# A gated-shift MLP block on one core: tiles 10 and 11 transposed by DMA, and the order around the second and third pair of tiles rewritten

## The chip, the cores and the metric

The kernel runs on one core of one Trainium2 chip. The metric is the time of one execution on the device in microseconds (us); lower is better. The core has five instruction streams that run side by side and wait for each other by semaphores: TensorE (PE in the profile, its weight loads PEld), VectorE (DVE), ScalarE (ACT), GpSimd (POOL) and SyncE (SP). SP issues nearly all DMAs here, ScalarE the first three.

## The reference

The input x has 2048 rows of 512; all data is bfloat16. Cut to what matters:

```python
h  = gelu(layernorm(x) @ w1)                 # w1: 512 x 512
hs = concat(h[:, 0:128]   shifted down 1 row,
            h[:, 128:256] shifted up 1 row,
            h[:, 256:384] shifted down 2 rows,
            h[:, 384:512] shifted up 2 rows) @ w2   # zeros come in at the ends
x1 = x + hs
out = x1 + gelu(layernorm(x1) @ w3) @ w4     # w3: 512 x 1792, w4: 1792 x 512
```

## The kernel before, in words

The rows are dealt to 16 tiles of 128 rows so that row r is row r // 16 of tile r % 16 (line 183). A shift by one or two rows is then a step to a neighbouring tile: for tile t the second product reads quarter j=0 of h from tile t-1, j=1 from t+1, j=2 from t-2 and j=3 from t+2 (`window`, lines 229 to 242). The layer norm is split in steps on three engines: `st` (statistics, VectorE, line 291), `ag` (mean and variance, VectorE, 296), `rs` (reciprocal roots, GpSimd, 302) and `nm` (the normalised tile, VectorE, 311). Every product needs its input transposed.

Every operation is recorded with a name, an engine, and what it reads and writes. `arrange` (lines 38 to 82) then puts the operations of each engine into the order of a list of names written by hand (`firsts`, lines 662 to 676), and `emit` (84 to 169) derives the semaphore waits. Each engine executes its list in order, so an operation that waits holds back all that stand behind it on its engine. That is true of SP too: a DMA whose source isn't ready holds back the later DMAs of the list.

The names, with the tile's number t (of a pair, the first tile):

- `ldx`, `ldw1`, `ldw2`, `ldw3a`, `ldw3b`, `ldw4`: loads of tiles of x (128 KB each) and of parts of the weights. `ldw20` to `ldw23` are the four 128-row parts of w2, one for each j; `ldw3a0` to `ldw3a3` are 256 KB each.
- Tiles 0 to 5 take a way of their own: `tp` and `ev` transpose the raw x on TensorE (line 357) and copy it out of the matmul accumulator banks, PSUM, on ScalarE (366), `m1r` is the first product (405), `rc` copies it out (415), `cs` and `cse` make the column sums of w1 (393, 397), and `zr` (420) and `g1r` (426) apply the norm afterwards. `th` transposes their h by DMA (384).
- Tiles 6 to 15, in pairs: the normalised tiles are transposed. Pairs 6, 12 and 14 do this with one DMA each (`td0_6`, `td0_12`, `td0_14`, line 377, issued on SP), pairs 8 and 10 with eight TensorE transposes (`tp8`, `tp10`, line 357) and a copy on ScalarE (`ev8`, `ev10`, line 366). Then `m1p` is the first product of a pair (16 matmuls of 256 columns, line 437, into two PSUM banks), and `g1p` or, for each tile of pair 10 alone, `g1s` is its GELU on ScalarE (447, 452).
- `m2` is the second product of a tile, four matmuls of 512 columns, one for each j (463). For tiles 8 to 13 it is cut in parts (`m2s`, line 478): parts ending in a letter come first, the part without a letter last. `x1` adds x on VectorE (488).
- The second layer: `st1`, `ag1`, `rs1`, `nm1` as above, `td1` transposes by DMA (377), `m3` and `m3h` are the third product (496, 520), `g2` and `g2h` its GELU (507, 531), `m4` the fourth (539), `fin` the last sum (551). It starts with tiles 8 to 11, the first call being `m3h_0_0_0` in banks 4 and 5.

The eight PSUM banks are given out by hand. Before the change m1p of the pairs 6, 8, 10, 12 and 14 uses the banks 2-3, 4-5, 0-1, 2-3 and 4-5, and the second products of the tiles 8 to 15 use 6, 7, 0, 1, 6, 7, 2, 3. `cs` is in bank 4, the `m1r` of tiles 4 and 5 in banks 0 and 1.

Of the kernel before, what the change touches and what calls it, by code (L numbers as in the profile page):

```python
# [5 lines left out]
P = 128  # L6
ACT_F = mybir.ActivationFunctionType
ALU = mybir.AluOpType
BF16 = mybir.dt.bfloat16
F32 = mybir.dt.float32  # L10
# [16 lines left out]
class Program:  # L27
# [7 lines left out]
    def add(self, eng, name, fn, reads=(), writes=(), dma=False):  # L35
        self.ops.append(Op(name, eng, fn, reads, writes, dma))
# [135 lines left out]
def bass_standalone__mixer_s_mlp__prompt_kernel(nc: bass.Bass, x, w1, w2, w3, w4, out):  # L172
# [3 lines left out]
    NT = S // P  # L176
# [9 lines left out]
    POS = {t: k for k, t in enumerate(ORDER)}  # L186

    with ExitStack() as es:
# [18 lines left out]
        st9 = sb("st9", [P, 2 * NT, 9], F32)  # L207
        mv = sb("mv", [P, 2 * NT, 2], F32)
        rstd = sb("rstd", [P, 2 * NT], F32)
        nmean = sb("nmean", [P, 2 * NT], F32)  # L210
        nbias = sb("nbias", [P, 2 * NT], F32)
        neghalf = sb("neghalf", [P, 4], F32)
        warm = sb("warm", [P, 1], F32)
        o_sb = sb("o_sb", [P, 4, D], BF16)
# [32 lines left out]
        add = pr.add  # L247
# [34 lines left out]
        def src_of(layer, t):  # L282
            return (x_sb, ("x", t)) if layer == 0 else (x1_sb, ("x1", t))

        def dst_of(layer, t):
            return (xn, t, ("xn", t), 0) if layer == 0 else (x1n, POS[t] % 8, ("x1n", POS[t] % 8), t)
# [19 lines left out]
        def norm(layer, t):  # L306
            src, r = src_of(layer, t)
            dst, k, dr, tag = dst_of(layer, t)
            i = layer * NT + (t if layer == 0 else POS[t])
            add("dve", f"nm{layer}_{t}",  # L310
                lambda e: e.tensor_scalar(dst[:, k, :], src[:, t, :], mv[:, i, 0:1], rstd[:, i : i + 1],  # L311
                                          ALU.subtract, ALU.mult),
                reads=[(r, 0), (("mv", i), 0), (("rstd", i), 0)], writes=[(dr, tag)])

        def nbias_op(layer, t, n):
            i = layer * NT + (t if layer == 0 else POS[t])
            add("dve", f"nb{layer}_{t}",
                lambda e: e.scalar_tensor_tensor(nbias[:, i : i + n], mv[:, i : i + n, 0], -1.0,
                                                 rstd[:, i : i + n], ALU.mult, ALU.mult),
                reads=[(("mv", i + k), 0) for k in range(n)] + [(("rstd", i + k), 0) for k in range(n)],  # L320
                writes=[(("nb", i + k), 0) for k in range(n)])

        def norm_act(layer, t):
            src, r = src_of(layer, t)
            dst, k, dr, tag = dst_of(layer, t)
            i = layer * NT + (t if layer == 0 else POS[t])
            add("act", f"na{layer}_{t}",
                lambda e: e.activation(dst[:, k, :], src[:, t, :], ACT_F.Identity,
                                       bias=nbias[:, i : i + 1], scale=rstd[:, i : i + 1]),
                reads=[(r, 0), (("nb", i), 0), (("rstd", i), 0)], writes=[(dr, tag)])  # L330

        def negmean(layer, t, n):
            i = layer * NT + (t if layer == 0 else POS[t])
            add("dve", f"ng{layer}_{t}",
                lambda e: e.tensor_scalar(nmean[:, i : i + n], mv[:, i : i + n, 0], -1.0, None, ALU.mult),
                reads=[(("mv", i + k), 0) for k in range(n)], writes=[(("nmean", i + k), 0) for k in range(n)])

        def norm_pool(layer, t):
            src, r = src_of(layer, t)
            dst, k, dr, tag = dst_of(layer, t)  # L340
            i = layer * NT + (t if layer == 0 else POS[t])
            add("pool", f"np{layer}_{t}",
                lambda e: e.tensor_scalar(dst[:, k, :], src[:, t, :], nmean[:, i : i + 1], rstd[:, i : i + 1],
                                          ALU.add, ALU.mult),
                reads=[(r, 0), (("nmean", i), 0), (("rstd", i), 0)], writes=[(dr, tag)])


        def tp(t, n, b, raw):
            src = x_sb if raw else xn
            rd = [(("x", i), 0) if raw else (("xn", i), 0) for i in range(t, t + n)]  # L350

            def f(e):
                ins = None
                for i in range(n):
                    for c in range(DC):
                        o = 1024 * b + (i * DC + c) * P
                        ins = e.transpose(psb[:, o : o + P], src[:, t + i, P * c : P * (c + 1)], ident[:])  # L357
                return ins

            add("pe", f"tp{t}", f, reads=rd + [("ident", 1)], writes=bres(b, 1, f"tp{t}"))  # L360
# [107 lines left out]
            add("pe", f"m2_{t}", f, reads=rd, writes=bres(b, 1, f"m2_{t}"))  # L468


        def m2s(t, b, js, first, last):
            wins = [(j, window(j, t)) for j in js]
            assert all(w[2] is None for _, w in wins)

            def f(e):
                ins = None
                for n, (j, w) in enumerate(wins):
                    ins = e.matmul(bank(b), hTf[:, w[0] : w[0] + P], w2_sb[:, j, :],  # L478
                                   start=first and n == 0, stop=last and n == len(js) - 1)
                return ins  # L480

            name = f"m2_{t}" if last else f"m2_{t}a" if first else f"m2_{t}b"
            add("pe", name, f, reads=[W2[j] for j in js] + [(("hT", w[1]), 0) for _, w in wins],
                writes=bres(b, 1, name))

# [100 lines left out]
        load_w1(2, "act")  # L586
        load_w1(3, "sp")
        load_x(1, 1, "act")
        for t, n in ((6, 1), (7, 1), (2, 1), (8, 1), (3, 1), (9, 1), (10, 1), (4, 1), (11, 1), (5, 1), (12, 2), (14, 1), (15, 1)):
            load_x(t, n)  # L590
        for c in range(DC):
            load_w2(c)
# [19 lines left out]
        for t in range(R, NT, 2):  # L612
            roots(0, t, 2)
        for t in range(R, NT):
            if t in ():
                nbias_op(0, t, 1)
                norm_act(0, t)
            else:
                norm(0, t)
        for t in range(R, NT, 2):  # L620
            if t in (8, 10):
                tp(t, 2, 6 + t // 2 % 2, False)
                ev(t, 2, 6 + t // 2 % 2)
            else:
                tdma(0, t, 2)
        for t, b in ((6, 2), (8, 4), (10, 0), (12, 2), (14, 4)):
            m1p(t, b)
            if t == 10:
                g1s(t, b, 0)
                g1s(t, b, 1)  # L630
            else:
                g1p(t, b)
        load_w("w4", w4_sb, w4, after=[(("x1T", 12), 0)])
        even = [((0, 1, 2), True, False), ((3,), False, True)]
        odd = [((0, 2), True, False), ((1, 3), False, True)]
        M2PARTS = {8: even, 9: [odd[0], ((1,), False, False), ((3,), False, True)], 10: even, 11: odd, 12: even, 13: odd}
        for t, b in ((8, 6), (9, 7), (10, 0), (11, 1), (12, 6), (13, 7), (14, 2), (15, 3)):
            for js, first, last in M2PARTS.get(t, ()):
                m2s(t, b, js, first, last)
            if t not in M2PARTS:  # L640
                m2(t, b)
            x1(t, b)
# [9 lines left out]
        for t in (8, 10):  # L652
# [8 lines left out]

        firsts = {}
        firsts["pe"] = """wu tp0 cs0 cs1 m1r01 m1r02 tp1 m1r03 m1r0 cs2 tp2 m1r12 m1r1 cs tp3 m1r2 tp4 m1r3 tp5 m1r4 m1r5 tp8 m1p6
            tp10 m1p8 m1p10 m2_8a m2_9a m2_8 m2_9b m2_9 m2_10a m2_11a m1p12 m1p14 m2_10 m2_11 m2_12a m2_13a m2_12 m2_13 m2_14 m2_15""".split()
        firsts["act"] = """ldw10 ldw12 ldx1 table ev0 ev1 ev2 rc0 ev3 rc1 ev4 rc2 ev5 rc3 rc4 rc5 ev8 cse g1p6 ev10 g1p8 g1s10 g1s11
            g1r0 g1r1 g1p12 g1p14 g2h_0_0_0 g2h_0_0_4 g1r2 g1r3 g2h_0_0_8 g2h_0_0_12 g1r4 g1r5""".split()
        firsts["dve"] = """pada padb padc padd pade padf st0_0 st0_6 st0_7 ag0_6 ag0_7
            st0_8 nm0_6 nm0_7 st0_9 ag0_8 ag0_9 st0_10 st0_11 nm0_8 nm0_9 ag0_10 ag0_11
            st0_12 st0_13 nm0_10 nm0_11 ag0_12 ag0_13 st0_14 nm0_12 nm0_13 st0_15 ag0_14 ag0_15 st0_1 ag0_0 ag0_1
            nm0_14 nm0_15 zr0 zr1 x1_8 x1_9 st1_8 st1_9 ag1_8 ag1_9 st0_2 nm1_8 nm1_9 st0_3 ag0_2 ag0_3 x1_10 x1_11 st1_10  # L670
            st1_11 ag1_10 ag1_11 x1_12 nm1_10 nm1_11 x1_13 x1_14 x1_15 zr2 zr3 st0_4 st0_5 ag0_4 ag0_5 zr4 zr5
            st1_12 st1_13 ag1_12 ag1_13""".split()
        firsts["pool"] = """ident0 ident1 neghalf stz ste rs0_6 rs0_8 rs0_10
            rs0_12 rs0_14 rs0_0 rs1_8 rs0_2 rs1_10""".split()
        firsts["sp"] = """ldx0 ldw11 ldw13 ldx6 ldx7 ldx2 ldx8 ldx3 ldx9 ldx10 ldx4 ldx11 ldx5 ldx12 td0_6 ldx14 ldx15 ldw20 ldw21 ldw22 ldw23 td0_12 ldw3a0 ldw3a1 td0_14
            ldw3a2 ldw3a3 th_0 td1_8 ldw3b0 ldw3b1 ldw3b2 ldw3b3 td1_10 th_2 th_4 td1_12 td1_14 ldw4""".split()

        slots = [4, 0, 2]
# [111 lines left out]
```

## Time and profile before

| What | Value |
|---|---|
| Three runs | 137.01 us median (136.91 to 137.36) |
| The profiled execution | 136.84 us, its span 134.9 us |
| Granted TensorE clock | 1.000 |
| TensorE busy | 131.8 us, 98% of the span |
| VectorE, ScalarE, GpSimd busy | 57.9, 47.6, 12.4 us |
| Data read from and written to HBM | 6.82 MB and 2.10 MB |

The profile is of one execution. Its span runs from the first to the last instruction; the time of an execution is a little longer. Times in the timelines count from the start of the span. In a row of the chain or of a timeline the first number is the start and the second the length, both in us; "x8" is the number of instructions merged into the row, and the text in brackets is the idle time ahead of the row and what ended it. A line number of the profile is that of the kernel; where a helper records several operations, they share a line and are told apart by time and order. For a DMA the profile gives the time that its issue took on the queue's engine and, in another view, the time from issue to landing.

### The profile page before, as it was taken

Reading aid. Unit: us, or ns where it says so; the run is one execution under the profiler, and the core shown is the slowest. Engines: PE = TensorE matmul, PEld = TensorE weight load, DVE = VectorE, ACT = ScalarE, POOL = GpSimd, SP = SyncE. Lnnn points to the kernel's source line nnn. Section 1 sums busy time; section 2 is a strip of 40 time slices with the busy share of each in tenths; the row PEclk is TensorE's granted clock in tenths of the full one; section 3 lists DMA queues with packets and bytes.
Section 4 is the critical chain, followed back from the end, with each engine's and each line's share of the span. In section 5 each row is a group of like instructions: output and inputs, shape, how many; then the busy total and the mean of one; then the engine's idle time right before and its main releaser. Section 6 shows DMA issues by size and latency. Waiting matters only on the chain.

```text
span 134.9 us, 1823 instructions
## 1 busy us (share of the span) xinstructions
PE 131.8 (98%) x737; PEld 69.8 (52%) x737; DVE 57.9 (43%) x135; ACT 47.6 (35%) x58; POOL 12.4 (9%) x25
## 2 busy tenths in 40 slices
PE   7999999999999999999999999999999999999993
PEld 2356867568885444444444444444444444444452
DVE  0499979999866786772222000122200002322222
ACT  3489873407963025551000555200066630000000
POOL 2023422220420012220000000000000000000000
PEclk9999999999999999999999999999999999999999
DMA  3988589774466973444112000011110001111121
GB/s 104 332 264 189 151 228 251 132 222 83 77 119 119 290 256 66 92 78 78 39 48 70 3 0 0 0 39 39 39 39 5 0 0 39 39 39 39 41 78 41
DMA packets 23512, 12.70 MB, mean 94 GB/s; under 512 B 15696, under 2 KB 22864, under 8 KB 23504
## 3 DMA queue, kind: packets, MB, share of 16 engines
q1 hardware_dynamic: 22928, 12.16, 35.8%
q10 hardware_dynamic: 576, 0.43, 1.1%
q8 instruction: 6, 0.10, 0.3%
q14 instruction: 2, 0.02, 0.0%
HBM read 6.82 MB, written 2.10 MB: 66 GB/s over the span
## 4 chain that ended last, share of the span: by engine, by line
PE 98%; DVE 0%; issue 0%
PE ps L539 36%; PE ps L496 27%; PE ps L520 9%; PE ps L437 6%; PE ps L463 6%; PE ps L405 4%; PE ps L478 4%; PE ps L562 2%; PE ps L357 2%; PE ps L393 1%; DVE o_sb L551 0%
## 5 line engine op out<-in xcount | busy, mean ns | idle before, releaser
L539 PE MATMUL ps<-w_sb,h2T 128*128 128x512 bf16 (+2 forms) x238 | 48.9, 367 | 0.0
L507 ACT ACTIVATE h2T<-ps 128x1024 bf16<-128x1024 f32 x21 | 21.5, 1023 | 46.2 <-PE ps L496 46.2
L551 DVE TENSOR_TENSOR o_sb<-ps,x_sb 128x512 bf16<-128x512 f32 (+2 forms) x17 | 11.2, 660 | 61.2 <-PE ps L539 61.2
L496 PE MATMUL ps<-x1nT,w_sb 128*128 128x512 bf16 x168 | 36.8, 379 | 0.0
L539 PEld LDWEIGHTS ps<-w_sb,h2T 128*128 128x128 bf16 x238 | 22.7, 98 | 26.0
L496 PEld LDWEIGHTS ps<-x1nT,w_sb 128*128 128x128 bf16 x168 | 16.5, 98 | 19.8
L291 DVE BATCH_NORM_STATS2 st<-x_sb 128x6 f32<-128x512 bf16 x32 | 20.6, 676 | 4.1 <-DMA x_sb<-in_x_dram 4.1
L302 POOL TENSOR_TENSOR rstd<-mv,neghalf 128x2 f32<-128x2 f32 x16 | 11.5, 718 | 46.6 <-DVE mv L296 46.5
L520 PE MATMUL ps<-x1nT,w_sb 128*128 128x256 bf16 x112 | 12.4, 273 | 0.0
L488 DVE TENSOR_TENSOR x_sb<-ps,x_sb 128x512 bf16<-128x512 f32 x16 | 10.6, 685 | 3.1 <-PE ps L463 2.1
L520 PEld LDWEIGHTS ps<-x1nT,w_sb 128*128 128x128 bf16 x112 | 11.0, 98 | 1.5
L531 ACT ACTIVATE h2T<-ps 128x1024 bf16<-128x1024 f32 (+1 forms) x8 | 7.1, 913 | 6.6 <-PE ps L520 6.6
L437 PE MATMUL ps<-xnT,w_sb 128*128 128x256 bf16 x80 | 9.2, 273 | 0.0
L463 PE MATMUL ps<-w_sb,hTf 128*128 128x512 bf16 x40 | 9.0, 379 | 0.0
L437 PEld LDWEIGHTS ps<-xnT,w_sb 128*128 128x128 bf16 x80 | 7.7, 98 | 1.2
L311 DVE TENSOR_SCALAR x1n<-x_sb,mv,rstd 128x512 bf16<-128x512 bf16 x16 | 5.9, 410 | 5.3 <-POOL rstd L302 5.3
L366 ACT ACTIVATE xnT<-ps 128x512 bf16<-128x512 bf16 (+1 forms) x8 | 5.6, 702 | 2.5 <-PE ps L357 2.4
L463 PEld LDWEIGHTS ps<-w_sb,hTf 128*128 128x128 bf16 x40 | 3.9, 98 | 4.5
L405 PE MATMUL ps<-w_sb,xnT 128*128 128x512 bf16 x24 | 6.2, 381 | 0.0
L478 PE MATMUL ps<-w_sb,hTf 128*128 128x512 bf16 x24 | 5.5, 379 | 0.0
L447 ACT ACTIVATE hTf<-ps 128x1024 bf16<-128x1024 f32 x4 | 4.1, 1023 | 3.4 <-PE ps L437 3.4
L296 DVE BATCH_NORM_AGGREGATE mv<-st 128x2 f32<-128x9 f32 x32 | 4.9, 184 | 0.0
(28 smaller groups left out, 37.2 us busy)
## 6 DMA issues: line engine op xcount, KB each, us to landing
out_dram<-o_sb SPq DMA_DIRECT2D x15, 128.0 KB, 1.8
w_sb<-in_w_dram SPq DMA_DIRECT2D x1, 1792.0 KB, 8.1
x_sb<-in_x_dram SPq DMA_DIRECT2D x13, 128.0 KB, 3.5
w_sb<-in_w_dram SPq DMA_DIRECT2D x4, 256.0 KB, 3.8
w_sb<-in_w_dram SPq DMA_DIRECT2D x6, 128.0 KB, 3.3
w_sb<-in_w_dram SPq DMA_DIRECT2D x4, 192.0 KB, 3.0
w_sb<-in_w_dram ACTq DMA_DIRECT2D x2, 128.0 KB, 3.5
x_sb<-in_x_dram SPq DMA_DIRECT2D x1, 256.0 KB, 3.5
```

The costliest lines, as they stand in the source:

```text
L291: add("dve", f"st{layer}_{t}", lambda e: e.bn_stats(st9[:, i, 0:6], src[:, t, :]), reads=[(r, 0)], writes=[(("st6", i), 0)])
L302: lambda e: e.tensor_tensor(rstd[:, i : i + n], mv[:, i : i + n, 1], neghalf[:, 0:n], ALU.pow),
L405: ins = e.matmul(bank(b), xnT[:, t, c, :], w1_sb[:, c, :], start=(c == 0), stop=(c == DC - 1))
L437: ins = e.matmul(dst, w1_sb[:, c, P * fc : P * (fc + 1)], xnT[:, t : t + 2, c, :], start=(c == 0), stop=(c == DC - 1))
L463: ins = e.matmul(bank(b), hTf[:, c0 : c0 + P], w2_sb[:, j, :], start=(j == 0), stop=(j == DC - 1))
L478: ins = e.matmul(bank(b), hTf[:, w[0] : w[0] + P], w2_sb[:, j, :], start=first and n == 0, stop=last and n == len(js) - 1)
L488: lambda e: e.tensor_tensor(x1_sb[:, t, :], bank(b), x_sb[:, t, :], ALU.add),
L496: ins = e.matmul(bank(b), w3_sb[:, c, P * fc : P * (fc + 1)], x1nT[:, 4 * q : 4 * q + 4, c, :], start=(c == 0), stop=(c == DC - 1))
L507: lambda e: e.activation(h2T[:, fc : fc + 2, q % 2, :], src, ACT_F.Gelu_apprx_tanh),
L520: ins = e.matmul(dst, w3_sb[:, c, P * (fc + i) : P * (fc + i + 1)], x1nT[:, t : t + 2, c, :], start=(c == 0), stop=(c == DC - 1))
L539: ins = e.matmul(ps[:, 512 * b : 512 * b + c1 - c0], h2T[:, fc, q % 2, P * i : P * (i + 1)], w4_sb[:, fc, c0:c1], start=(fc == 0), stop=(f ...
L551: lambda e: e.tensor_tensor(o_sb[:, k % 4, c0:c1], ps[:, 512 * b : 512 * b + c1 - c0], x1_sb[:, t, c0:c1], ALU.add),
```

## The change

Pair 10 is transposed by a DMA (`td0_10`) instead of `tp10` and `ev10`. On TensorE the parts of the second products of tiles 8 and 9, and the first part of tile 10, are put around `m1p10`, some ahead of it; tile 9's is now in four parts. Tiles 10 and 11 accumulate in banks 4 and 5, and `m1p14` in banks 0 and 1. On ScalarE `cse` moves ahead of `rc5`. On VectorE `st0_15` moves ahead of `nm0_12`, `st0_2`, `st0_3` and their `ag` ahead of `x1_8`, `zr2` ahead of `nm1_8` and `zr3` ahead of `x1_10`. On GpSimd `rs0_2` moves ahead of `rs1_8`. On SP x tile 4 is loaded ahead of tile 10, tiles 14 and 15 are loaded by one DMA, w2's parts come in the order 0, 2, 1, then `td0_10` and `td0_12`, and only then part 3. Helpers for norms on other engines, which no tile used, are removed with their buffers.

```diff
-        nmean = sb("nmean", [P, 2 * NT], F32)
-        nbias = sb("nbias", [P, 2 * NT], F32)
...
-        def m2s(t, b, js, first, last):
+        def m2s(t, b, js, name, first, last):
...
-            name = f"m2_{t}" if last else f"m2_{t}a" if first else f"m2_{t}b"
...
-        for t, n in ((6, 1), (7, 1), (2, 1), (8, 1), (3, 1), (9, 1), (10, 1), (4, 1), (11, 1), (5, 1), (12, 2), (14, 1), (15, 1)):
+        for t, n in ((6, 1), (7, 1), (2, 1), (8, 1), (3, 1), (9, 1), (10, 1), (4, 1), (11, 1), (5, 1), (12, 2), (14, 2)):
...
-            if t in ():
-                nbias_op(0, t, 1)
-                norm_act(0, t)
-            else:
-                norm(0, t)
+            norm(0, t)
         for t in range(R, NT, 2):
-            if t in (8, 10):
-                tp(t, 2, 6 + t // 2 % 2, False)
-                ev(t, 2, 6 + t // 2 % 2)
+            if t == 8:
+                tp(t, 2, 6, False)
+                ev(t, 2, 6)
             else:
                 tdma(0, t, 2)
-        for t, b in ((6, 2), (8, 4), (10, 0), (12, 2), (14, 4)):
+        for t, b in ((6, 2), (8, 4), (10, 0), (12, 2), (14, 0)):
             m1p(t, b)
...
-        even = [((0, 1, 2), True, False), ((3,), False, True)]
-        odd = [((0, 2), True, False), ((1, 3), False, True)]
-        M2PARTS = {8: even, 9: [odd[0], ((1,), False, False), ((3,), False, True)], 10: even, 11: odd, 12: even, 13: odd}
-        for t, b in ((8, 6), (9, 7), (10, 0), (11, 1), (12, 6), (13, 7), (14, 2), (15, 3)):
-            for js, first, last in M2PARTS.get(t, ()):
-                m2s(t, b, js, first, last)
+        M2PARTS = {8: ((0, 2), (1,), (3,)), 9: ((2,), (0,), (1,), (3,)), 10: ((0, 2), (1,), (3,)),
+                   11: ((0, 2), (1, 3)), 12: ((0, 1, 2), (3,)), 13: ((0, 2), (1, 3))}
+        for t, b in ((8, 6), (9, 7), (10, 4), (11, 5), (12, 6), (13, 7), (14, 2), (15, 3)):
+            parts = M2PARTS.get(t, ())
+            for n, js in enumerate(parts):
+                last = n == len(parts) - 1
+                m2s(t, b, js, f"m2_{t}" + ("" if last else "abc"[n]), n == 0, last)
...
         firsts["pe"] = """wu tp0 cs0 cs1 m1r01 m1r02 tp1 m1r03 m1r0 cs2 tp2 m1r12 m1r1 cs tp3 m1r2 tp4 m1r3 tp5 m1r4 m1r5 tp8 m1p6
-            tp10 m1p8 m1p10 m2_8a m2_9a m2_8 m2_9b m2_9 m2_10a m2_11a m1p12 m1p14 m2_10 m2_11 m2_12a m2_13a m2_12 m2_13 m2_14 m2_15""".split()
+            m1p8 m2_8a m2_9a m1p10 m2_8b m2_9b m2_10a m2_8 m2_9c m2_9 m2_10b m2_11a m1p12 m1p14 m2_10 m2_11 m2_12a m2_13a m2_12 m2_13 m2_14 m2_15""".split()
-        firsts["act"] = """ldw10 ldw12 ldx1 table ev0 ev1 ev2 rc0 ev3 rc1 ev4 rc2 ev5 rc3 rc4 rc5 ev8 cse g1p6 ev10 g1p8 g1s10 g1s11
+        firsts["act"] = """ldw10 ldw12 ldx1 table ev0 ev1 ev2 rc0 ev3 rc1 ev4 rc2 ev5 rc3 rc4 cse rc5 ev8 g1p6 g1p8 g1s10 g1s11
...
-            st0_12 st0_13 nm0_10 nm0_11 ag0_12 ag0_13 st0_14 nm0_12 nm0_13 st0_15 ag0_14 ag0_15 st0_1 ag0_0 ag0_1
-            nm0_14 nm0_15 zr0 zr1 x1_8 x1_9 st1_8 st1_9 ag1_8 ag1_9 st0_2 nm1_8 nm1_9 st0_3 ag0_2 ag0_3 x1_10 x1_11 st1_10
-            st1_11 ag1_10 ag1_11 x1_12 nm1_10 nm1_11 x1_13 x1_14 x1_15 zr2 zr3 st0_4 st0_5 ag0_4 ag0_5 zr4 zr5
+            st0_12 st0_13 nm0_10 nm0_11 ag0_12 ag0_13 st0_14 st0_15 nm0_12 nm0_13 ag0_14 ag0_15 st0_1 ag0_0 ag0_1
+            nm0_14 nm0_15 zr0 zr1 st0_2 st0_3 ag0_2 ag0_3 x1_8 x1_9 st1_8 st1_9 ag1_8 ag1_9 zr2 nm1_8 nm1_9 zr3 x1_10 x1_11 st1_10
+            st1_11 ag1_10 ag1_11 x1_12 nm1_10 nm1_11 x1_13 x1_14 x1_15 st0_4 st0_5 ag0_4 ag0_5 zr4 zr5
...
-            rs0_12 rs0_14 rs0_0 rs1_8 rs0_2 rs1_10""".split()
-        firsts["sp"] = """ldx0 ldw11 ldw13 ldx6 ldx7 ldx2 ldx8 ldx3 ldx9 ldx10 ldx4 ldx11 ldx5 ldx12 td0_6 ldx14 ldx15 ldw20 ldw21 ldw22 ldw23 td0_12 ldw3a0 ldw3a1 td0_14
+            rs0_12 rs0_14 rs0_0 rs0_2 rs1_8 rs1_10""".split()
+        firsts["sp"] = """ldx0 ldw11 ldw13 ldx6 ldx7 ldx2 ldx8 ldx3 ldx9 ldx4 ldx10 ldx11 ldx5 ldx12 td0_6 ldx14 ldw20 ldw22 ldw21 td0_10 td0_12 ldw23 ldw3a0 ldw3a1 td0_14
             ldw3a2 ldw3a3 th_0 td1_8 ldw3b0 ldw3b1 ldw3b2 ldw3b3 td1_10 th_2 th_4 td1_12 td1_14 ldw4""".split()
```

More of the change, by code (lines that the diff above doesn't have):

```diff
@@ L313, in norm @@
                 reads=[(r, 0), (("mv", i), 0), (("rstd", i), 0)], writes=[(dr, tag)])
[L315 to L345, printed above, removed]
         def tp(t, n, b, raw):
```

## The prediction

> **What bounds the kernel now.** I read the page's busy shares first, then the chain that ended last, then the timelines of SP, VectorE and ScalarE from 8 to 30 us, then the landing of each DMA, asked for one issue at a time.
>
> ```profile
> PE 131.8 (98%) x737; PEld 69.8 (52%) x737; DVE 57.9 (43%) x135; ACT 47.6 (35%) x58; POOL 12.4 (9%) x25
> ```
>
> ```profile
> 12.29 0.45 PE ps L357 x8
> 12.74 1.75 PE ps L437 x16
> 14.49 0.45 PE ps L357 x8
> 14.93 3.50 PE ps L437 x32
> 18.44 2.81 PE ps L478 x13
> 21.24 3.49 PE ps L437 x32
> ```
>
> The chain (start, length, engine, line, count) is TensorE alone from its first matmul to the end. In these rows it never waits: 13 matmuls of 512 columns in 2.81 us are 0.216 us each, the same as in the last 126 (24.22 us). So the time falls only by TensorE work taken away, and rises by any wait put into its order. The second row of eight at L357 (14.49) is tp10, the transposes that the change removes.
>
> ```profile
> 8.94 1.34 SPq L377 DMA_TRANSPOSE xnT<-xn  x1
> 10.33 1.04 SPq L274 DMA_DIRECT2D x_sb<-in_x_dram  x2
> 11.42 1.85 SPq L574 DMA_DIRECT2D w_sb<-in_w_dram  x4
> 15.25 1.56 SPq L377 DMA_TRANSPOSE xnT<-xn  x1
> 16.85 1.05 SPq L580 DMA_DIRECT2D w_sb<-in_w_dram  x2
> 17.95 1.24 SPq L377 DMA_TRANSPOSE xnT<-xn  x1
> ```
>
> SP issues in order, and a transpose at the head holds all behind it until its tiles are normalised: td0_12 goes out at 15.25, when nm0_13 has ended (below).
>
> ```profile
> 12.79 0.72 DVE L311 TENSOR_SCALAR xn<-x_sb,mv,rstd 128x512 bf16<-128x512 bf16 x2
> 13.61 0.65 DVE L291 BATCH_NORM_STATS2 st<-x_sb 128x6 f32<-128x512 bf16 x1
> 14.49 0.73 DVE L311 TENSOR_SCALAR xn<-x_sb,mv,rstd 128x512 bf16<-128x512 bf16 x2 [0.24 <-POOL rstd L302]
> 15.14 0.69 DVE L291 BATCH_NORM_STATS2 st<-x_sb 128x6 f32<-128x512 bf16 x1
> ```
>
> Last, us from issue to landing (last number) of ldx14, ldw20, ldw23, td0_12, ldw3a0 and td0_14, in that order:
>
> ```profile
> x_sb<-in_x_dram SPq DMA_DIRECT2D x1, 128.0 KB, 2.9
> w_sb<-in_w_dram SPq DMA_DIRECT2D x1, 128.0 KB, 2.6
> w_sb<-in_w_dram SPq DMA_DIRECT2D x1, 128.0 KB, 3.2
> xnT<-xn SPq DMA_TRANSPOSE x1, 3.1
> w_sb<-in_w_dram SPq DMA_DIRECT2D x1, 256.0 KB, 3.0
> xnT<-xn SPq DMA_TRANSPOSE x1, 4.1
> ```
>
> **Part 1: what goes.** Eight transposes of 128 columns leave TensorE: 0.45 us by the chain. ev10, 1.02 us of ScalarE, goes too and was never waited for. "All norms on VectorE" removes code that no tile reached (its condition is an empty tuple), and two unused buffers: nothing. Tile 4 ahead of 10: tp4 waited for its load (0.31 us in the chain, where four transposes otherwise take 0.22), so up to 0.09 us more. x10 then takes the old place of x4, issued at 5.45 and landed 3.6 later, at 9.05; st0_10 starts at 9.66, so that is hidden. The most to be had is 0.45 + 0.09 = 0.54 us.
>
> **Part 2: m1p8 and m1p10.** m1p8 can start at 14.49. It needs ev8 and, for bank 4, cse. On ScalarE cse now stands before rc5: rc4 ends at 12.18, cse and rc5 take 0.49 each (the spacing of rc3 and rc4), so ev8 ends near 14.1 instead of 13.84. Hidden, by 0.4 us. m1p8 takes 1.75 to 16.24, then m2_8a and m2_9a (three matmuls, 0.65) to 16.89; g1p6 (done 15.54) and ldw22 (now second of the W2 loads, issued about 11.4, in by about 14.8 at 3.4) are in time. m1p10 now waits for td0_10 instead of ev10. nm0_11 ends at 13.51, issue 13.54, landing 3.1 to 3.2 later: 16.65 to 16.75. The loads ahead of it could hold it: td1_8 landed 1.27 us after th_0 where it was queued behind it, and ldw22 of before landed at 15.67; 15.67 + 1.27 = 16.94. So m1p10 starts between 16.8 and 17.05 with 0.1 for the wait to pass, where the old order without its transposes would have it at 16.89. A stall here costs 0 to 0.15 us; I take 0.05. The order behind m1p10 covers ScalarE: g1s10 ends 0.58 after m1p10 and four matmuls (0.86) stand between.
>
> **Part 3: the last W2 load.** ldw23 went out at 12.85 and landed at 16.05. Now it stands behind td0_12 on SP, and behind td0_10 too. Its first user is m2_8, the j=3 part, seven matmuls after m1p10: 16.89 + 1.75 + 4 x 0.216 = 19.50. td0_12 itself is later: st0_15 now runs before nm0_12, so the two statistics end at 14.85 instead of the norm starting at 14.49; nm0_13 ends at 15.50 instead of 15.22 and td0_12 is issued at 15.53. Its issue takes 1.24 to 1.56 us (the three rows above), so ldw23 goes out between 16.8 and 17.15; middle 16.95. The nearest landings are ldx14, the 128 KB load straight behind a transpose, 2.9; ldw20, 2.6; ldw3a0, of 256 KB straight behind td0_12, 3.0; the longest of a 128 KB W2 load, 3.4. I take 2.8, nearest to the first two: 19.75, and 0.1 for the wait: 19.85. TensorE waits 0.35 us at m2_8. Against the profiled run that is 19.85 - 19.95 = -0.10 (19.95 being the old kernel's time after the same work). The ends: 16.8 + 2.6 + 0.1 = 19.5, no wait, -0.45; 17.15 + 3.4 + 0.1 = 20.65, +0.70.
>
> **Part 4: what is late next.** td0_14 slips from 17.95 to 16.95 + 0.57 + 2 x 0.47 = 18.5, ldw23 being added ahead of it. It needs the two W3 loads ahead of it to land: at 3.3 after issue as in before, w3a1 (issued 18.0) is in at 21.3, with ldw23's 128 KB ahead of it perhaps 21.5; plus 1.27 gives 22.6 to 22.8, plus 0.1. m1p14 stood at 22.99, so this allows -0.3 to -0.1. At 4.1 after 18.5, the row's own duration, it is 22.7. th_0 landed 3.8 us after td0_14, so now near 26.5; m2_14 needs it at 27.11 less the gain. x1_8 on VectorE starts near 20.1 instead of 19.77, since two statistics (1.28) and their sums now come before it, and zr2 (0.7) before nm1_8: td1_8 issues near 24.4 instead of 24.05, lands near 27.5, and m3h needs it at 28.8. Hidden by 1.2 us. x1_10 and x1_11 free banks 4 and 5 for the first m3h at 26.3, hidden by 2.4. All later work is the same TensorE stream, so the shift at m1p14 is carried to the end.
>
> **Sum.** The shift is the latest of three arrivals: td0_10 about -0.40, ldw23 -0.10, td0_14 -0.3 to -0.1. I take -0.10 us: 0.54 taken away and 0.44 given back as waits. The profiled execution took 136.84 us (span 134.9 and 1.9 around it): 136.74. The median of the three runs shown is 137.01, 0.17 above it, so on that scale 136.9.
>
> [...]
>
> **The rivals.**
> - *Nothing waits* (faster). ldw23 lands in 2.6 after a short issue of 1.24, and td0_10 in 3.1: -0.45, so 136.56 on the median's scale; with tp4's share 136.47. For it: ldw20's 2.6. Against it: ldx14, which stood in the very place, took 2.9. It must be in by 19.4. Chance 0.18.
> - *The transpose holds the queue no longer than a load* (faster). With td0_12 landing in ldw20's 2.6 instead of 3.1, ldw23 behind it lands 0.5 sooner, 19.25, and is not waited for; the time is again 136.56. [...] Against it: all three transposes of xn took 3.1 or more. Chance 0.04.
> - *td0_12 is backed up* (slower). If td0_10 holds the rings as the W3 loads held td0_14, td0_12 takes 4.1 and not 3.1: it lands at 15.53 + 4.1 = 19.63, ldw23 about 1.1 behind it (ldx14 landed 13.24, td0_6 12.14), with 0.1 at 20.83: +0.88, 137.9. It decides for slower once ldw23 is in after 20.26. For it: td0_14's 4.1 and th_0's 5.1. Against it: those had 512 KB just ahead, and td0_10 should be in by 17. Chance 0.16.
> - *Forecast*: ldw23 or td0_14 gives back most of the gain. Chance 0.62.
>
> **How the numbers follow.** 0.3%, 0.41 us, is about what a measurement of this kernel can tell from no change; the largest possible gain, 0.54, barely exceeds it. Faster: 0.18 + 0.04 = 0.22. Slower: 0.16. Within: 0.62. Range: down to the floor of the faster rivals, 137.01 - 0.54 = 136.47, and 0.1 for the spread of the runs shown (136.91 lowest): 136.4. Up to the late end of ldw23, 137.01 + 0.70 = 137.7, less the thinnest part: 137.6.
>
> **What would show it.** In the chain: no L357 row at 14.49; 16 + 16 matmuls at L437 parted by three of L478; a wait of 0.2 to 0.5 us on W2's DMA at L478 near 19.5, or on td0_14 at L437 near 22.5. ldw23 issued near 17.0, td0_14 near 18.5. It is wrong if no TensorE wait shows after 14 us (then -0.45), if td0_10 stalls m1p10 by over 0.2, if td0_12 takes over 3.6 to land, or if a wait shows after 28 us.

## The result and the profile after

The changed kernel is slower: 138.30 us median (137.72 to 138.93 in the executions compared) against 137.00 us; the ratio is 1.0093 with a 95% interval of 1.0064 to 1.0123. The prediction said 136.9, within 0.3%, and a range up to 137.6. The profiled execution took 138.30 us, its span is 136.4 us, 1.5 us more than before.

The page first: TensorE is busy for 0.5 us less than before, as the eight transposes are gone, but the chain is no longer its alone.

```profile
PE 131.3 (96%) x729; PEld 69.3 (51%) x729; DVE 57.8 (42%) x135; ACT 46.6 (34%) x57; POOL 12.8 (9%) x25
...
PE 83%; DMA 8%; DVE 4%; SPq 1%; issue 1%; POOL 1%
```

The chain of the changed kernel in the stretch that answers to the rows of before (start, length, what). Its lines are the old ones moved: L403 is the first product of a pair (L437 before), L444 the parts of the second (L478), L343 the DMA transpose (L377), L539 a w2 load (L574).

```profile
16.67 0.28 SPq L343
16.95 0.05 issue
17.00 4.12 DMA w_sb<-in_w_dram
21.11 0.14 issue
21.25 1.46 PE ps L444 x6
22.70 3.49 PE ps L403 x32
```

In these rows the end is set by SP's issue of td0_12, then by ldw23, which lands 4.12 us after its issue at 17.00, then by TensorE. m1p12 and m1p14 (the last row) started at 21.24 before and start at 22.70 now: 1.46 us of the span's 1.5. Behind it the chain has the rows of before, as long as before.

TensorE's timeline shows where it waits:

```profile
16.71 1.91 PE L403 MATMUL ps<-xnT,w_sb 128*128 128x256 bf16 x16
18.46 1.03 PE L444 MATMUL ps<-w_sb,hTf 128*128 128x512 bf16 x4
21.25 1.46 PE L444 MATMUL ps<-w_sb,hTf 128*128 128x512 bf16 x6 [1.76 <-DMA w_sb<-in_w_dram]
```

m1p10, then the four matmuls that the order puts behind it, then 1.76 us of nothing ahead of m2_8. SP's timeline and the us to landing (last number) of td0_10, td0_12 and ldw23, in that order, say why. The first row of SP holds two issues, td0_10's at 13.52 and td0_12's, from 15.72 to 16.95:

```profile
13.52 3.43 SPq L343 DMA_TRANSPOSE xnT<-xn  x2
17.00 1.52 SPq L539 DMA_DIRECT2D w_sb<-in_w_dram  x1
```

```profile
xnT<-xn SPq DMA_TRANSPOSE x1, 3.0
xnT<-xn SPq DMA_TRANSPOSE x1, 4.4
w_sb<-in_w_dram SPq DMA_DIRECT2D x1, 128.0 KB, 4.1
```

td0_10 landed as forecast. td0_12, issued at 15.72, took 4.4 us where 3.1 was expected, and ldw23 behind it 1.5 us to issue and 4.1 to land.

What held td0_12 is seen in the view of the DMA queues over a short window: bytes moved in 40 equal slices, each packet counted in the slice in which it starts, and the queues' packets. Before, from 15.0 to 18.0 us (0.075 us a slice):

```profile
GB/s 273 260 96 55 246 27 27 27 0 0 0 0 0 0 0 0 0 0 0 68 177 236 218 225 205 239 177 188 191 263 201 215 225 222 215 158 55 17 0 0
...
q8 instruction: 1, 0.02, 2.0%
```

After, from 16.5 to 19.5 us:

```profile
GB/s 0 0 218 0 0 68 181 229 208 208 201 208 171 164 55 17 7 0 0 0 0 7 7 7 7 14 7 10 10 10 7 10 126 280 294 287 287 297 456 300
...
q8 instruction: 1, 0.02, 3.0%
```

The lone slice of 218 or 246 GB/s is one 16 KB packet of the queue that the page calls instruction. Its time is 2.0% or 3.0% of 16 engines' 3 us, that is 1.0 or 1.4 us of one engine. Before, it starts at 15.4, when only the last packets of the loads still move (27 GB/s), and is over before td0_12's bytes, which flow without a break from 16.4 to 17.8. After, it starts at 16.69 and ends at 18.13; td0_12's bytes begin at 16.9, stop at 17.6, trickle from 18.1, when the fetch is over, at 7 to 14 GB/s against some 210 before, and flow again from 18.9, at 280 to 297 GB/s. I call this packet the fetch below.

### The profile page after: what moved, and what is told of

It reads as the page before. It is cut to its first block, busy times and chain, and to the rows that moved or that the text cites. A ratio compares the mean times of both kernels' runs of the same rounds, so it can differ in the third digit from the quotient of the medians.

```text
span 136.4 us, 1807 instructions
## 1 busy us (share of the span) xinstructions
PE 131.3 (96%) x729; PEld 69.3 (51%) x729; DVE 57.8 (42%) x135; ACT 46.6 (34%) x57; POOL 12.8 (9%) x25
## 4 chain that ended last, share of the span: by engine, by line
PE 83%; DMA 8%; DVE 4%; SPq 1%; issue 1%; POOL 1%
PE ps L504 35%; PE ps L461 27%; PE ps L485 9%; PE ps L429 6%; DMA x_sb<-in_x_dram 5%; DMA w_sb<-in_w_dram 3%; PE ps L444 3%; DVE st L289 3%; PE ps L403 3%; DVE xn L309 1%; DVE mv L294 1%; SPq L535 1%; SPq L343 1%; POOL rstd L300 1%; SPq L272 0%
## 5 line engine op out<-in xcount | busy, mean ns | idle before, releaser
L504 PEld LDWEIGHTS ps<-w_sb,h2T 128*128 128x128 bf16 x238 | 22.8, 98 | 25.9
L461 PEld LDWEIGHTS ps<-x1nT,w_sb 128*128 128x128 bf16 x168 | 16.4, 98 | 19.8
L403 PE MATMUL ps<-xnT,w_sb 128*128 128x256 bf16 x80 | 9.2, 273 | 0.0
L403 PEld LDWEIGHTS ps<-xnT,w_sb 128*128 128x128 bf16 x80 | 7.8, 98 | 1.3 <-DMA xnT<-xn 0.2
L444 PE MATMUL ps<-w_sb,hTf 128*128 128x512 bf16 x24 | 5.8, 379 | 1.8 <-DMA w_sb<-in_w_dram 1.8
L332 ACT ACTIVATE xnT<-ps 128x512 bf16<-128x512 bf16 (+1 forms) x7 | 4.7, 665 | 2.5 <-PE ps L323 2.5
```

Source lines behind the costliest of these rows:

```text
L403: ins = e.matmul(dst, w1_sb[:, c, P * fc : P * (fc + 1)], xnT[:, t : t + 2, c, :], start=(c == 0), stop=(c == DC - 1))
L461: ins = e.matmul(bank(b), w3_sb[:, c, P * fc : P * (fc + 1)], x1nT[:, 4 * q : 4 * q + 4, c, :], start=(c == 0), stop=(c == DC - 1))
L504: ins = e.matmul(ps[:, 512 * b : 512 * b + c1 - c0], h2T[:, fc, q % 2, P * i : P * (i + 1)], w4_sb[:, fc, c0:c1], start=(fc == 0), stop=(f ...
```

## The experiments

**Theory 1**: the loss is two waits on DMAs that the change put on TensorE's path, ldw23 and td0_10, and a fetch in flight holds a transpose for about 1.3 us. **Theory 2**: a transpose issued close behind another is slow by itself. **Rival 3**: the rewritten orders of VectorE, ScalarE and the second products cost the time. Ratios are to the kernel before, run beside.

**ldw23 early again** (two runs, e1_w2_early and e8_w2_early_again).

```diff
-ldw20 ldw22 ldw21 td0_10 td0_12 ldw23
+ldw20 ldw22 ldw21 ldw23 td0_10 td0_12
```

> The changed kernel with ldw23 back ahead of td0_10 on SP, nothing else moved. Theory 1: the 1.8 us wait at m2_8 is that load's lateness, so it goes; td0_12 is still held in flight (about 4.4 us to landing), and td0_14, behind it, makes m1p14 wait 0.2 to 0.6 us: 136.6 to 137.1. Theory 2 (a transpose close behind another takes longer by itself): the same time here. Rival 3 (the time is lost in the order on VectorE, ScalarE or TensorE): stays near 138.3.

> A second look at the changed kernel with ldw23 ahead of td0_10, whose first profile was of one of its shorter executions (136.9, where the median was 138.07). If this look falls on a longer one: by theory 1 a transpose is held longer or at another place than in the first (td0_10 or td0_14 4 us or more, and m1p10 or m1p14 waits for it); if no transpose is later than in the first look, theory 1 doesn't explain the longer executions.

Measured: 1.0060 (1.0031 to 1.0089), median 138.07. The executions compared fall in two groups, three from 136.71 to 136.90 and seven from 137.94 to 138.63. The two profiles are of one of each, 136.90 and 138.07. Rows of the chain of the shorter:

```profile
13.29 3.54 DMA xnT<-xn
16.83 0.05 issue
16.88 1.92 PE ps L403 x16
18.80 2.21 PE ps L444 x10
```

and of the longer:

```profile
13.66 4.62 DMA xnT<-xn
18.29 0.05 issue
18.33 1.92 PE ps L403 x16
20.25 2.21 PE ps L444 x10
```

In both, the wait at m2_8 is gone (all ten parts run as one row), as expected. In the shorter the fetch started at 16.3 and held td0_12 (4.3 us to landing), for which nobody waits any more. In the longer it started at 15.7, on td0_10's packets: td0_10 took 4.6 us, td0_12 3.4, and m1p10 started 1.45 us later. The window of the longer from 15.0 to 18.0 shows the break; nothing moves from 16.4 to 16.8, where the fetch ends (15.7 and 1.1 us long):

```profile
GB/s 246 263 239 246 198 222 212 246 218 454 177 181 184 171 199 96 28 20 4 0 0 0 0 0 7 10 51 154 102 34 24 7 14 10 4 31 266 280 297 294
```

So ldw23's lateness is one part, and what remains in the longer profile is td0_10, held; that it is the same in the other long executions is likely by their times, but they weren't profiled. The expected 136.6 to 137.1 held only for the few.

**The fetch moved earlier** (e2_waits24, e3_waits40): 48 and 80 waits ahead of tp0 for what is long reached, put down as 24 and 40 instructions of two waits each.

```diff
+                    if op.name == "tp0":
+                        for _ in range(48):
+                            objs[e].wait_ge(sems["pool"], 2)
                     ins = op.fn(objs[e])
```

> The changed kernel with 24 more instructions on TensorE's queue ahead of tp0, each only waiting for semaphores that have long been reached, in a stretch where TensorE waits for x anyway. They move no work; they only make the queue's instruction fetch fall earlier. Theory 1 (a fetch in flight beside a transpose holds the transpose for 1.3 to 1.5 us): the fetch that started at 16.69 now starts near 15, on td0_10's packets (14.6 to 16.1), so td0_10 takes about 4.4 us, m1p10 waits about 1.1 us, td0_12 is not held again, m2_8 no longer waits: 137.5 to 138.1. Theory 2 (a transpose close behind another is slow by itself): td0_10 3.0, td0_12 4.4, m2_8 waits 1.8 us, 138.3.

> The same with 40 such instructions. Theory 1: the fetch starts near 13 to 14; if it is over before td0_10's packets at 14.6, no transpose is held, td0_12 takes 3.1 us, ldw23 is in by 19.8 to 20.2 and m2_8 waits 0.3 to 0.6 us: 136.7 to 137.2; if it still meets td0_10, 137.5 to 138.1 as with 24. Theory 2: td0_12 4.4 us, 138.3.

With 24, measured: 1.0047 (1.0030 to 1.0063), 137.79. The fetch was found at 14.1 instead of 16.7. The landings of td0_10, td0_12 and ldw23:

```profile
xnT<-xn SPq DMA_TRANSPOSE x1, 3.7
xnT<-xn SPq DMA_TRANSPOSE x1, 3.1
w_sb<-in_w_dram SPq DMA_DIRECT2D x1, 128.0 KB, 3.1
```

The window from 14.0 to 17.0 has the fetch in its second slice (14.14, 0.96 us long), and now it is td0_10's bytes that break off, from 15.4 to 16.1:

```profile
GB/s 300 437 137 55 14 27 27 0 0 72 191 225 218 205 225 198 198 171 61 20 14 14 0 14 14 17 20 17 48 259 280 283 290 297 216 17 7 0 0 0
```

Two transposes 2.4 us apart, and the second takes 3.1: theory 2 falls. The hold moved with the fetch, to the last loads and td0_10 (landed at 17.20 instead of 16.55). It was shorter than expected, 3.7 us instead of 4.4, and m1p10 waited 0.45 us instead of 1.1. ldw23, issued at 17.14, still came at 20.23, and m2_8 started at 20.36; the expectation that m2_8 would not wait was wrong. (The profile puts this wait of 0.34 us down to ScalarE's GELU of tile 11, which ended 0.05 us after the load came; m2_8 reads tile 10, which was done at 19.8.) So the time fell in its range by another sum than the one written down. With 40, 1.0183 (1.0158 to 1.0208): the waits delayed tp0 itself by 2 us (5.95, where the warm-up ends at 3.92), so the time says nothing on the theories. Its fetch, at 16.1, fell between the two transposes, and td0_12 took 3.0.

**The place of ldw23 alone** (e4_before_w2_late): the kernel of before with one edit.

```diff
-ldw20 ldw21 ldw22 ldw23 td0_12
+ldw20 ldw22 ldw21 td0_12 ldw23
```

> The kernel of before with only w2's loads in the changed order 0, 2, 1, and part 3 behind td0_12. Its fetch (15.37) is over before td0_12's packets. Theory 1: td0_12 takes 3.1 us, ldw23 goes out at 16.85 and lands near 19.7, so m2_8 (19.52) waits 0.2 to 0.4 us, and td0_14 and m1p14 may add 0.3: 137.1 to 137.5. If the place of the load is enough by itself: m2_8 waits over 1 us, 138 or more.

Measured: 1.0027 (1.0011 to 1.0043), 137.39. The fetch came at 14.95 and took 0.97 us; ldw23 was issued at 16.70, behind td0_12, and landed 3.3 later; m2_8 started at 20.11 instead of 19.52. Of these 0.59 us 0.25 is the wait for the load, and 0.34 TensorE had lost ahead of it. As theory 1 expected: with no fetch beside it (it was over at 15.9) the place of this load costs some 0.4 us by the medians (0.15 to 0.59 by the interval).

**td0_14 ahead of W3, and other shifts of the fetch** (e5_early_both, e6_early_both_shift, e7_w2_early_shift).

```diff
-td0_10 td0_12 ldw23 ldw3a0 ldw3a1 td0_14        # e5, e6
+ldw23 td0_10 td0_12 td0_14 ldw3a0 ldw3a1
-warmup("wu", 7, 5)                              # e6, e7; 512 columns each
+warmup("wu", 20, 5)                             # 176 columns each, and 6 empty instructions
```

> The changed kernel with ldw23 ahead of td0_10, and td0_14 ahead of the first two W3 loads. Its executions, like those of the kernel with ldw23 early alone (136.7 to 138.8), tell whether td0_14 is what is late in the longer ones. If it is, all executions here come near 136.6 to 136.9, since td0_14 lands near 21.5 and m1p14 wants it at 22.5. If td0_10 or td0_12 is what is late (held by the instruction fetch), the spread stays: some near 136.7, most near 138.

> The same, with TensorE's warm-up of 7 matmuls of 512 columns done as 20 of 176 columns and 6 empty waiting instructions behind it: 32 more instructions in about the same time, which makes TensorE's instruction fetch start near 13.3 instead of 16.3, ahead of td0_10's packets. If the fetch is what holds the transposes, td0_10 and td0_12 both take 3.0 to 3.3 us, nothing waits behind m1p10, and the time is 136.4 to 136.8, the 0.45 us that the removed transposes are worth. If the fetch isn't the cause, as the kernel without this edit.

> The changed kernel with ldw23 ahead of td0_10 and the same shift of the fetch, td0_14 in its changed place. Fetch the cause: td0_12 3.0 to 3.3 us, 136.5 to 137.0, and the executions closer together than without the shift. Not the cause: 138 for most.

Measured: e5 1.0053 (1.0020 to 1.0087), again six executions from 136.85 to 137.17 and five from 138.37 to 138.82, so td0_14 isn't what is late. e6 1.0092 (1.0071 to 1.0114) and e7 1.0073 (1.0053 to 1.0093): the shift missed its aim. The fetch was found at 15.6 (e6, in its longest execution, 139.81) and 14.4 (e7), not at 13.3; td0_10 took 5.0 and 4.6 us. In e7 it met the loads ahead of td0_10 (ldw23 landed 4.8 us after issue), and td0_10 was late with them. By its time alone e7 came out as written for a fetch that isn't the cause (138 for most); since in neither the fetch got out of the way, neither tests it. They speak against the shift as a remedy.

**The fetch moved later** (e9_fewer36, e10_w2_early_fewer36, e11_before_fewer18).

```diff
                 for i in range(n):
+                    if t in (0, 1, 2, 3, 4, 5):     # e11: (3, 4, 5)
+                        ins = e.matmul(bank(b), ident[:], src[:, t, :], start=True, stop=True)
+                        continue
...
-            src = psb[:, 1024 * b : 1024 * b + n * D]
+            src = bank(b) if t in (0, 1, 2, 3, 4, 5) else psb[:, 1024 * b : 1024 * b + n * D]
```

> The changed kernel with 36 fewer TensorE instructions ahead of tp8 in the same TensorE time: the four transposes of 128 columns of each of tiles 0 to 5 are one matmul of 512 columns with the identity, so tiles 0 to 5 go into the first product untransposed and the output isn't the reference's. TensorE's instruction fetch then comes some 2 us later, near 18.5 to 19, behind td0_12's packets. Theory 1 (a fetch in flight holds a transpose, and the place of ldw23 costs only its ordinary landing): td0_10 3.0 to 3.2 us, td0_12 3.1, ldw23 in at 19.8 to 20.2, m2_8 waits 0.3 to 0.6, 136.7 to 137.2. If the place of ldw23 and the second transpose are the cause without the fetch: td0_12 4.4 and 138.3 as without this edit.

> The same with ldw23 ahead of td0_10. Theory 1: nothing is held and nothing stands in front of w2's last part, m2_8 doesn't wait, m1p10 waits 0 to 0.4 us for td0_10 behind ldw23, the time is 136.4 to 136.8, and the executions are close together. If something else in the change costs time: 137.5 to 138.2, as most executions of the kernel with ldw23 early.

> The kernel of before with 18 fewer TensorE instructions in the same way (tiles 3 to 5 untransposed, the output not the reference's): its fetch, 15.37 in the profile of before, should come near 16.4, on td0_12's packets (16.3 to 17.9). Theory 1: td0_12 takes 4.2 to 4.5 us in place of 3.1, though nothing of the change is in this kernel; td0_14 lands near 23.2 and m1p14 waits 0.2 to 0.5 us: 137.1 to 137.5. If the hold needs a second transpose close ahead: td0_12 3.1 us, 137.0.

Measured: e9 1.0087 (1.0060 to 1.0114), the time of the changed kernel. The fetch moved later, but to 18.1, not past td0_12: its window from 17.0 to 20.0 has the fetch's slice at 18.05 and the break from 18.6 to 19.7, in the tail of td0_12 in place of its head.

```profile
GB/s 0 0 31 150 215 236 222 218 208 205 205 225 195 212 427 205 177 177 178 100 82 14 14 137 55 68 0 75 61 24 10 7 10 10 10 7 10 164 314 396
```

td0_12 took 4.4 and ldw23 3.8. The 4.4 and the time are also the numbers written down for a cause without the fetch; since the fetch still fell on td0_12, the time can't part the two, and only the place of the break speaks for the fetch. e10 1.0052 (1.0024 to 1.0080), in the range written down for another cost: the fetch at 19.1 met the stragglers of td0_12 and the W3 loads, td0_14 landed at 23.26 and m1p14 waited for it. e11 1.0046 (1.0012 to 1.0081): its fetch came at 15.7, again too early for td0_12 (3.3 us), and nothing follows from its longer executions, which weren't profiled. The three misses have one reading: the changed kernel leaves gaps between its transfers that are shorter than a fetch of 0.9 to 1.6 us (0.7 us ahead of td0_12's bytes, 16.1 to 16.85), so the fetch falls on something; a place where it costs nothing was not found, unless it is that of e3, where TensorE was late for another reason.

**One part undone: pair 10 on TensorE** (e12_pe10, e13_pe10_w2_early).

```diff
-            if t == 8:
+            if t in (8, 10):
...
-            m1p8 m2_8a m2_9a m1p10
+            tp10 m1p8 m2_8a m2_9a m1p10
-rc5 ev8 g1p6 g1p8
+rc5 ev8 g1p6 ev10 g1p8
-td0_10 td0_12            # e13: ldw23 ahead of td0_12
+td0_12
```

> The changed kernel with one part undone: pair 10 is transposed on TensorE again (tp10 ahead of m1p8, ev10 behind g1p6), all other orders as changed, ldw23 behind td0_12. Theory 1: no DMA between TensorE's first product of pair 10 and its transposed tiles, the rings are idle ahead of td0_12, so it takes 3.1 to 3.4 us, ldw23 lands near 20.0 and m2_8, at 19.9 to 20.0 in TensorE's order, waits 0 to 0.4 us: 136.9 to 137.5, and the executions lie closer together than the changed kernel's. If the rest of the order costs the time: 138 or more.

> The same with ldw23 ahead of td0_12. Theory 1: both edits that put a DMA on TensorE's path are undone, so it is the kernel of before with the orders of VectorE, ScalarE and of the second products: 136.8 to 137.1. If those orders cost something by themselves: above 137.3.

Measured: e12 1.0045 (1.0032 to 1.0059), 137.62, 0.1 above what was expected and its executions close together (137.25 to 137.73); e13 1.0011 (0.9999 to 1.0024), 137.14, 0.04 above its range and below the 137.3 of the other case. In e12's chain the load is still what TensorE waits for, though the fetch (14.8, 0.96 us long) has ended 1.5 us before td0_12's issue ends at 17.26:

```profile
17.30 3.17 DMA w_sb<-in_w_dram
20.48 0.14 issue
20.61 1.46 PE ps L444 x6
```

Four kernels make a table (ratio to before):

| | ldw23 early | ldw23 behind td0_12 |
|---|---|---|
| pair 10 on TensorE | 1.0011 (e13) | 1.0045 (e12) |
| pair 10 by DMA | 1.0060 (e1) | 1.0093 (the change) |

The late load costs 0.0034 and 0.0033, that is 0.46 us, in either row; the DMA for pair 10 costs 0.0049 and 0.0048, 0.66 us, in either column, though it frees 0.45 us of TensorE. Each of these differences is uncertain by 0.002 to 0.004, so that they agree to the last digit is luck, and the late load's in the lower row alone is not clear of nothing. What is left of the change, the other orders, costs 0.0011 with an interval that reaches to none: rival 3 falls. No version beat the kernel before beyond its interval.

The 0.66 us aren't td0_10's wait alone. Undoing it also gives TensorE 16 instructions back (eight transposes and their weight loads), and the fetch moves with them: it starts at 14.8 to 15.4 in the profiles of three kernels that transpose pair 10 on TensorE (before, e4, e12) and at 15.7 to 16.7 in those of the changed kernel, e1 and e8. So the change itself moved the fetch onto its transposes. No run parts the price of the DMA from that of this move.

## Why the prediction was wrong, point by point

**Part 1** was right on the transposes: TensorE is busy for 0.5 us less. The 0.09 us at tp4 didn't come: with tile 4 ahead of 10, tp4 started at 9.09 as before (9.08). x3 landed later in this execution, and tp3 waited for it.

**Part 2** was right in the profiled execution and wrong as a price. td0_10 was issued at 13.52 and landed after 3.0; TensorE's weight load for m1p10 waited 0.21. But I bounded td0_10 by the loads ahead of it alone, 0 to 0.15 us. With 0.1 us of slack, its real price is what holds it in other executions, 1.45 us in the second profile with ldw23 early. By the table the DMA, with the fetch that came later by it, loses 0.66 us net, where the sum had it gain 0.4; the sum has no term for the fetch.

**Part 3 is the step that failed.** ldw23 was issued at 17.00, near the forecast (16.95), in part by luck: td0_12 went out 0.19 later than summed, as tiles 14 and 15 now come by one load and st0_14 started only when it had landed (13.74), and its issue took 1.23, the short end. ldw23 landed 4.1 us later, not 2.8, outside the ends of 2.6 and 3.4: m2_8 waited until 21.25, not 19.85. The row taken, ldx14 behind td0_6, was a transpose that nothing held. Unheld, the same place measured 3.1 to 3.3 (e2, e4, e12), nearer the end than my middle, with 0.14 and not 0.1 for the wait. So of the 1.4 us between 19.85 and 21.25 some 0.4 is a landing taken too short, 0.9 the hold that the sum put at nothing, and 0.1 the rest. The prediction's own sign for a hold, td0_12 over 3.6 us, came (4.4). The sentence that puts m2_8 seven matmuls after m1p10 is a slip: three of the seven stand ahead of it, and the sum counts four behind it, as the order has it.

**Part 4** was right that later work is covered: td0_14 landed at 23.6 and m1p14 came at 24.4, td1_8 at 29.4 ahead of m3h at 30.3.

**The rivals.** What happened is the slower one in its place and size: td0_12 took 4.4 (the rival had 4.1) and the time rose by 1.3 us (0.88). Its reason was wrong. It let td0_10's backlog hold td0_12, and I counted against it that td0_10 should be in by 17; it was in at 16.55, and td0_12 was held all the same. The trace of before held a clue: its th_0 took 5.1, and I put it down to the loads ahead. The window over th_0 has an instruction packet too (of the queue q14, 0.3 us long), and a break of 1.1 us in the bytes behind it; whether the one made the other wasn't tried. Its td0_14, 4.1, is no such clue: from 17.0 to 22.8 that trace has no instruction packet, so the W3 loads ahead stay its likely reason.

Where no fetch met it (before, e2, e3), td0_12 landed 3.0 to 3.1 us after its issue, not in the 2.6 of the second rival; the 128 KB loads of w2 before took 2.6 to 3.4. Its issue on SP took 1.56 us before and 1.23 in the change, that of a load of w2 before 0.43. What decided were the held ones, 3.7 to 4.6 (e2, the change, e1, e8, e9).

**What is shown, and what isn't.** Shown: the two DMAs cost what the table says; in each window above of a held transpose its bytes break off 0.5 to 1.3 us after a fetch starts and are back at over 250 GB/s 0.6 to 1.0 us after it ends, and editing TensorE's instructions alone moved the fetch (16.7 to 14.1 and 18.1, where two executions of one kernel differ by 0.6) and the hold with it. That the packet brings TensorE's instructions is my reading of these moves; the trace names its queue only as instruction. Why a whole transfer breaks off when a packet takes one engine for 1.0 to 1.4 us isn't shown: the trace doesn't say which engine a packet ran on. A changed kernel with no fetch in this stretch wasn't reached, so what it would take without holds stays open.

## What to carry to other kernels

Price a DMA that is put on the path by its slack, not by its median landing: here a hold of some 1.3 us cost nothing with slack (td0_12 with ldw23 early) and nearly all of itself without (td0_10 in the longer execution). Before swapping an engine's work for a transfer, write down for each DMA around it when it lands and when it is wanted; the old order had 2.9 us for td0_12 and 3.5 for w2's last part, the new one 0.1 for td0_10 and less than none for that load. And undo each part alone: the profile put the whole wait on ldw23, while by the table the larger part of the loss came with pair 10's DMA. Work taken off TensorE also moved the fetch (14.8 to 15.4 with pair 10 on TensorE, 15.7 to 16.7 without); look where that falls.

## What the runs showed of the hardware

- A 16 KB instruction packet took 0.9 us (e6) to 1.6 us (e7) of one DMA engine in the stretch around 14 to 19 us, and the bytes of a DMA transpose in flight around it stood nearly still (0 to 20 GB/s against some 210) for 0.7 us (td0_10 in e2) and 1.3 us (td0_12 in the change).
- With 1,458 matmuls and weight loads on TensorE (the change), the queue q8 brought six such packets; the 48 waits of e2 ahead of tp0 moved the one at 16.69 to 14.14.
- ldw23, issued on SP while td0_12 was in flight and held (the change), took 1.52 us to issue; the loads of w2 and w3 before took 0.43 to 0.58.
- 32 more waits for a semaphore value already reached (80 in e3, 48 in e2) moved tp0 from 4.25 to 5.95, 0.053 us each.
